# GQA decode attention with a gated MLP: the first block of wo by its own transfers in mid-run

## The chip, the core and the metric

The kernel runs on one NeuronCore of a Trainium2 chip. The metric is the device time of one execution in microseconds. Before the change it is 678.9 us, the median of three runs (678.57 to 679.03). The profiled execution took 678.28 us.

## What is computed

One token for each of 8 sequences goes through grouped-query attention over a cache, and the result is gated by an MLP:

```python
xn = layernorm(x)                                   # x: 8 x 1 x 512
q  = xn @ wq                                        # 32 heads of 128
p  = softmax(q . k_cache * 128 ** -0.5)             # 8 kv heads, 4096 keys each
s  = (p @ v_cache) as 8 x 4096, @ wo                # wo: 4096 x 512
g  = silu(gmlp(xn))                                 # w_in, spatial gate, w_out
out = x + s * g
```

All data is float32. The k and v caches are 8 x 8 x 4096 x 128 each, so nearly all of the 290.85 MB that a run moves is cache. wo is read as 32 blocks (one for each query head) of 128 rows x 512.

## The kernel before

Three slots of 128 x 16384 float32 (A, B, C) take all large arrays in turn. SyncE (SP) issues nearly all loads: wq into B, then for each of the 8 kv heads the two halves of k into A and B (`load_k`, L572) and the two halves of v into C and B (`load_v`, L577 and L578). A load waits on SP until the tensor engine has read the slot's last contents. ScalarE (ACT) issues x and w_mlp at the start. GpSimd issues no transfer: in the loop over the heads it only copies one head's q into `qz` (L524), and each of these copies waits for the previous head's output to be stored (L620).

For one head, the scores of all sequences are matmuls into PSUM (L531); a softmax over 128 x 1024 follows on VectorE and ScalarE; then the values (L563), whose diagonal blocks VectorE picks and sums (L565, L566), and a small matmul that puts them together (L569). The tensor engine and VectorE run these heads as a hardware loop; the other engines' programs are written out. A recorder notes every instruction with the regions that it reads and writes, and works out the waits: a matmul that reads a loaded block waits for the transfers that wrote it.

At the end wo goes into slot A in seven pieces, listed in `WO_PIECES` by block numbers and issued by L582, one semaphore each. Blocks 0 to 27 are multiplied by `folded_wo` (L590) into four row groups of PSUM, block by block as the pieces land; VectorE copies the sum out (L634), 16 small matmuls fold the row groups (L639), and blocks 28 to 31 are multiplied straight into the result's shape by `direct_wo` (L598). The gate and x follow on VectorE (L644, L645), and SP stores the result (L646).

A transfer of 128 rows is spread over the core's 16 DMA engines.

Of the kernel before, what the change touches and what calls it, by code (L numbers as in the profile page):

```python
# [15 lines left out]
P = 128  # L16
B, D = 8, 512
HKV, REP, S, DH = 8, 4, 4096, 128
# [3 lines left out]
R = 32  # L22
# [5 lines left out]
HALF = B // 2  # L28
UNIT = 2 * G * 512
SLOT = HALF * UNIT  # L30
WO_PIECES = [(0, 14), (14, 22), (22, 25), (25, 28), (28, 30), (30, 31), (31, 32)]
FOLDED = 28
FOLD_AT = 29
X_PARTS = 2
# [1 line left out]
XW = D + 64  # L36
E = 2
W = P // E
BANK = 512


class Region:


    def __init__(self, ap):
# [10 lines left out]
        if str(ap.space) == "PSUM" or "PSUM" in str(ap.space):  # L56
            self.p0, self.p1 = 0, P
            banks = np.unique(at // BANK)
            at = (banks[:, None] * BANK + np.arange(BANK)[None, :]).reshape(-1)
        at = np.unique(at)  # L60
# [279 lines left out]
        return self.rec.add(self.eng, "tensor_tensor", (out, a, b), {"op": ALU.subtract})  # L340


def gqa_gmlp_decode(real, x, kT, v, wq, wo, w_mlp, out):
    nc = Recorder(real)

    def sb(name, shape, **kw):
        return real.alloc_sbuf_tensor(name, shape, F32, **kw).ap()
# [51 lines left out]
    def shift(t, i):  # L399
        lo = (E - 1 - i) * B  # L400
        return t[:, lo:lo + R]
# [19 lines left out]

    gate, xg, wb = sb("gate", [P, W]), sb("xg", [P, W]), sb("wb", [P, 2])
    px = scr[1][:, :W + 2]
    for i in range(E):
        for g in range(G):
            lo = g * P + i * W
            nc.tensor.matmul(px[R * g:R * (g + 1), :W], shift(same8, i)[:B], x_sb[:, lo:lo + W],
                             start=(i == 0), stop=(i == E - 1))
    nc.tensor.matmul(px[:, W:], ones, xs_sb[0:1, D:D + 2], start=True, stop=True)
    nc.vector.tensor_copy(xg, px[:, :W])  # L430
    nc.vector.tensor_copy(wb, px[:, W:])
# [85 lines left out]
    oT = sb("oT", [P, FOLDED // REP, REP, B])  # L517
# [63 lines left out]
    def load_wo(lo, hi):  # L581
        nc.sync.dma_start(slots["A"][:, lo * D:hi * D], wo[:, lo * D:hi * D])  # L582

    wo_sb = slots["A"].rearrange("p (m d) -> p m d", d=D)
    part, acc = sc[:, 0, :], sc[:, 1, :W]

    def folded_wo(lo, hi):
        for m in range(lo, hi):
            h, r = divmod(m, REP)
            nc.tensor.matmul(part[R * r:R * r + B, :], oT[:, h, r, :], wo_sb[:, m, :],  # L590
                             start=(m < REP), stop=(m >= FOLDED - REP))

    def direct_wo(lo, hi):
# [8 lines left out]
    def head(h):  # L602
        spread_q(h)
        for half, n in enumerate("AB"):
            scores(half, load_k(h, half, n))
        softmax()
        for half, n in enumerate("CB"):
            v_sb, rest = load_v(h, half, n, 1 if h == HKV - 1 and half else 0)
            for i in range(HALF):
                b = half * HALF + i  # L610
                values(b, v_sb[:, i], rest if b == B - 3 else None)
                if b > 0:
                    combine(b - 1)
        combine(B - 1)
        if h < FOLDED // REP:
            to = oT[:, h]
        else:
            m = h * REP - FOLDED
            to = oT_end[:, m:m + REP, (E - 1) * B:E * B]
        nc.stored = nc.scalar.activation(to, po.rearrange("p (b r) -> p r b", r=REP), AF.Copy)  # L620
# [2 lines left out]
    project_q(1)  # L623
    mlp()
    nc.meet("tensor")
    for h in range(HKV):
        with nc.round(h):
            head(h)

    for lo, hi in WO_PIECES:  # L630
        load_wo(lo, hi)
    folded_wo(0, FOLDED)
    part_sb = pbuf[:, :D]
    nc.vector.tensor_copy(part_sb, part)  # L634
# [46 lines left out]
```

## Time and profile before

| what | value |
|---|---|
| median of 3 runs | 678.9 us (678.57 to 679.03) |
| profiled execution | 678.28 us |
| its span | 677.0 us |
| data moved | 290.85 MB, 430 GB/s over the span |
| PE busy | 373.0 us (55%) |
| VectorE busy | 164.9 us (24%) |
| GpSimd busy | 4.3 us (1%) |
| DMA packets | 6229, of which 6048 on SP's queue, 176 on ACT's, 5 for instructions |

The span is the time from the first to the last instruction in the profile. "q1" is SP's queue and "q10" ACT's. A DMA share of 1.00 means that all 16 DMA engines were at work throughout a stretch; 0.25 is four of them. PEclk is the tensor engine's granted clock as a share of full speed. A row of the timeline gives start, duration, engine, line, and in brackets the idle time before it and what ended it.

### The profile page before, as it was taken

How to read it: one execution, taken by the hardware profiler on the slowest of the kernel's cores; microseconds unless marked ns; L12 is line 12 of the kernel's file. 1: busy time of each engine (PE TensorE's matmuls, PEld its weight loads, DVE VectorE, ACT ScalarE, POOL GpSimd, SP SyncE). 2: the span in 40 equal slices, each digit the busy share in tenths (PEclk: the TensorE clock that was granted, in tenths of full speed). 3: DMA queues.
4: the chain of work that ended last, by engine and by line, in shares of the span. 5: the costliest groups of instructions: out<-in, count | busy, mean ns of one | idle time of the engine just before them, and what ended most of it. 6: DMA issues, size and time to landing. Idle time of an engine off the chain costs nothing. (4 is left out here: it accounts for less than half of the span.)

```text
span 677.0 us, 5987 instructions
## 1 busy us (share of the span) xinstructions
PE 373.0 (55%) x2570; PEld 118.4 (17%) x2570; DVE 164.9 (24%) x261; ACT 15.0 (2%) x35; POOL 4.3 (1%) x22
## 2 busy tenths in 40 slices
PE   0084864536665464555755355655745456755676
PEld 0021321112111121111211021111211121211222
DVE  2014042301440033401421024400422024400361
ACT  0000000000000000000000000000000000000000
POOL 1000000000000000000000000000000000000000
PEclk9996877888776667878767678876667788776697
DMA  9999999999999999999999999999999999999997
GB/s 382 446 429 434 435 434 434 435 434 434 434 434 434 434 434 434 434 434 434 434 434 434 434 434 434 434 434 434 434 434 434 434 434 434 434 434 434 453 413 314
DMA packets 6229, 290.85 MB, mean 430 GB/s; under 512 B 832, under 2 KB 848, under 8 KB 1488
## 3 DMA queue, kind: packets, MB, share of 16 engines
q1 hardware_dynamic: 6048, 285.25, 97.4%
q10 hardware_dynamic: 176, 5.52, 1.9%
q8 instruction: 4, 0.07, 0.0%
q14 instruction: 1, 0.01, 0.0%
HBM read 290.74 MB, written 0.03 MB: 430 GB/s over the span
## 5 line engine op out<-in xcount | busy, mean ns | idle before, releaser
L531 PE MATMUL sc<-slot_B,qz 128*32 128x512 f32 x512 | 71.6, 722 | 71.3 <-PEq L531 71.3
L563 PE MATMUL o_ps<-slot_B,tbuf 128*16 128x512 f32 x512 | 75.0, 712 | 63.4 <-PEq L563 63.4
L531 PE MATMUL sc<-slot_A,qz 128*32 128x512 f32 x512 | 72.6, 731 | 44.7 <-PEq L531 44.7
L563 PE MATMUL o_ps<-slot_C,tbuf 128*16 128x512 f32 x512 | 77.3, 746 | 13.9 <-PEq L563 13.9
L565 DVE TENSOR_TENSOR o_all<-o_ps,diag 128x512 f32<-128x512 f32 x64 | 44.2, 691 | 136.4 <-DVEq L565 135.5
L535 DVE TENSOR_REDUCE nm<-sc 128x1 f32<-128x1024 f32 x8 | 9.8, 1224 | 264.1 <-DVEq L535 264.1
L566 DVE TENSOR_REDUCE o_sb<-o_all 128x128 f32<-128x512 f32 x64 | 67.7, 1058 | 9.3
L531 PEld LDWEIGHTS sc<-slot_B,qz 128*32 128x32 f32 x512 | 20.4, 130 | 122.3 <-issue 122.3
L531 PEld LDWEIGHTS sc<-slot_A,qz 128*32 128x32 f32 x512 | 20.5, 131 | 90.2 <-issue 90.2
L569 PE MATMUL po<-fold,o_sb 128*128 128x4 f32 x128 | 24.4, 261 | 18.5 <-PEq L569 17.0
L569 PEld LDWEIGHTS po<-fold,o_sb 128*128 128x128 f32 x128 | 20.1, 198 | 73.9 <-issue 73.9
L563 PEld LDWEIGHTS o_ps<-slot_B,tbuf 128*16 128x16 f32 x512 | 13.3, 105 | 91.3 <-issue 90.8
L563 PEld LDWEIGHTS o_ps<-slot_C,tbuf 128*16 128x16 f32 x512 | 15.7, 113 | 56.3 <-issue 56.0
L553 PE MATMUL scr<-ident,pbuf 128*128 128x128 f32 x64 | 15.5, 424 | 13.4 <-PEq L553 13.4
L440 PE MATMUL scr<-slot_B,xnT 128*32 128x512 f32 x64 | 8.9, 706 | 19.5 <-PEq L440 19.5
L553 PEld LDWEIGHTS scr<-ident,pbuf 128*128 128x128 f32 x64 | 12.5, 223 | 13.8 <-issue 13.8
L536 ACT ACTIVATE pbuf<-sc,nm 128x1024 f32<-128x1024 f32 x8 | 8.9, 1113 | 271.4 <-DVEq L535 271.4
L554 DVE COPY tbuf<-scr 128x512 f32<-128x512 f32 x16 | 11.1, 691 | 12.3 <-DVEq L554 12.3
L590 PE MATMUL sc<-slot_A,oT 128*8 128x512 f32 x56 | 9.6, 801 | 1.6 <-DMA slot_A<-in_wo 1.6
L539 PE MATMUL scr<-ident,nm 128*1 128x128 f32 x8 | 2.2, 270 | 13.6 <-PEq L539 13.6
L442 DVE TENSOR_SCALAR pbuf<-scr 128x512 f32<-128x512 f32 x2 | 1.4, 692 | 27.6 <-PE scr L440 27.6
L546 PE MATMUL scr<-wl,same 128*128 128x1 f32 x16 | 3.2, 272 | 8.0 <-PEq L546 8.0
(100 smaller groups left out, 76.8 us busy)
## 6 DMA issues: line engine op xcount, KB each, us to landing
slot_B<-in_v SPq DMA_DIRECT2D x1, 6144.0 KB, 25.9
slot_C<-in_w_mlp ACTq DMA_DIRECT2D x1, 5376.0 KB, 40.6
slot_A<-in_wo SPq DMA_DIRECT2D x1, 3584.0 KB, 37.0
slot_B<-in_v SPq DMA_DIRECT2D x1, 2048.0 KB, 28.9
slot_A<-in_wo SPq DMA_DIRECT2D x1, 2048.0 KB, 41.3
slot_A<-in_wo SPq DMA_DIRECT2D x2, 768.0 KB, 43.4
slot_A<-in_wo SPq DMA_DIRECT2D x1, 512.0 KB, 44.9
slot_A<-in_wo SPq DMA_DIRECT2D x2, 256.0 KB, 45.1
```

The source lines that it names most:

```text
L440: nc.tensor.matmul(pq[R * g:R * (g + 1), :], xnT[:, k, :], wq_sb[:, k, lo:lo + REP * DH], start=(k == 0), stop=(k == NK - 1))
L531: nc.tensor.matmul(sc[R * g:R * (g + 1), c, :], qz[:, b * R:(b + 1) * R], k_sb[:, i, c, g, :], start=(b == 0), stop=(b == B - 1))
L535: nc.vector.tensor_reduce(nm, sc, op=ALU.max, axis=AX.XY, negate=True)
L536: nc.scalar.activation(p.rearrange("p j s -> p (j s)"), sc.rearrange("p c s -> p (c s)"), AF.Exp, bias=nm, accum_out=l)
L546: nc.tensor.matmul(tot, same_all, wl, start=True, stop=True)
L553: nc.tensor.transpose(t[:, j * P:(j + 1) * P], p[:, 4 * c + j, :], ident)
L554: nc.vector.tensor_copy(pT[:, :, 4 * c:4 * c + 4].rearrange("p b j (g r) -> p (j g) b r", g=G), t.rearrange("p (m b r) -> p m b r", b=B, r ...
L563: nc.tensor.matmul(of[R * c:R * c + G * REP, :], pT[:, b, j, :], v_unit[:, j], start=(j < G), stop=(j >= J - G))
L565: nc.vector.tensor_mul(o_all[b % 2], o, diag[:, :, None].to_broadcast([P, G, DH]), after=after)
L566: nc.vector.tensor_reduce(o_sb[b % 2], o_all[b % 2].rearrange("p g d -> p d g"), op=ALU.add, axis=AX.X)
L569: nc.tensor.matmul(po[:, b * REP:(b + 1) * REP], o_sb[b % 2], fold, start=True, stop=True)
L590: nc.tensor.matmul(part[R * r:R * r + B, :], oT[:, h, r, :], wo_sb[:, m, :], start=(m < REP), stop=(m >= FOLDED - REP))
```

## The change

Block 0 of wo no longer comes with the first piece. It has a place of its own, `wo_0` (128 x 512), and is brought in by three transfers that are issued ahead of head 4: on GpSimd one of 7 rows and one of 119 rows (seven times 17), and on SP one of the last 2 rows. For the GpSimd transfers the host packs block 0 a second time, as the array `wo_first`: seven lines that hold 17 rows each and, behind them, one row as two halves set apart. In GpSimd's program the two transfers stand between the copy of q for head 3 and that for head 4; in SP's, the third stands between the last load of v of head 3 and the first load of k of head 4. `folded_wo` reads block 0 from its new place.

```diff
-WO_PIECES = [(0, 14), (14, 22), (22, 25), (25, 28), (28, 30), (30, 31), (31, 32)]
+WO_PIECES = [(1, 14), (14, 22), (22, 25), (25, 28), (28, 30), (30, 31), (31, 32)]
...
+SK, SR, SH = 7, 17, 4
...
+    def wo_block(m):
+        return wo_sb[:, m, :] if m else wo_0
+
...
-            nc.tensor.matmul(part[R * r:R * r + B, :], oT[:, h, r, :], wo_sb[:, m, :],
+            nc.tensor.matmul(part[R * r:R * r + B, :], oT[:, h, r, :], wo_block(m),
                              start=(m < REP), stop=(m >= FOLDED - REP))
...
+    wo_0 = sb("wo_0", [P, D])
+
+    def load_first():
+        half = D // 2
+        nc.gpsimd.dma_start(wo_0[:SK], wo_first[:, SR * D:].rearrange("k (a d) -> k a d", a=2)[:, :, :half])
+        nc.gpsimd.dma_start(wo_0[SK:SK + SK * SR], wo_first[:, :SR * D].rearrange("k (r d) -> k r d", d=D))
+        nc.sync.dma_start(wo_0[SK + SK * SR:], wo[SK + SK * SR:, :D])
+
     for h in range(HKV):
+        if h == SH:
+            load_first()
         with nc.round(h):
             head(h)
...
+    first = wo[:, :D]
+    halves = np.zeros((SK, 2, D), np.float32)
+    halves[:, :, :D // 2] = first[:SK].reshape(SK, 2, D // 2)
+    wo_first = np.concatenate([first[SK:SK + SK * SR].reshape(SK, SR * D), halves.reshape(SK, 2 * D)], axis=1)
```

## Rows read from the trace of the kernel before

**Rows 1.** The page, parts 1 to 3: busy time, 40 slices, queues (packets, MB, share).
```profile
PE 373.0 (55%) x2570; PEld 118.4 (17%) x2570; DVE 164.9 (24%) x261; ACT 15.0 (2%) x35; POOL 4.3 (1%) x22
...
DMA  9999999999999999999999999999999999999997
GB/s 382 446 429 434 435 434 434 435 434 434 434 434 434 434 434 434 434 434 434 434 434 434 434 434 434 434 434 434 434 434 434 434 434 434 434 434 434 453 413 314
...
q8 instruction: 4, 0.07, 0.0%
```

**Rows 2.** The chain of waits in order of time: start us, us, what.
```profile
626.28 36.99 DMA slot_A<-in_wo
...
663.32 9.63 PE sc L590 x56
...
675.14 0.23 DVE res L645
```

**Rows 3.** Stretches at the last landing: engines' busy time, PEclk, DMA share, GB/s.
```profile
672.25:672.50 0.25, 0.25 (x6) 0.00 (x0) 0.00 (x0) 0.00 (x0) 0.00 (x0) 1.00 0.98 385
672.50:672.75 0.25, 0.25 (x3) 0.00 (x0) 0.00 (x0) 0.00 (x0) 0.00 (x0) 1.00 0.61 230
672.75:673.00 0.25, 0.16 (x3) 0.00 (x0) 0.03 (x1) 0.00 (x0) 0.00 (x0) 1.00 0.34 131
673.00:673.25 0.25, 0.04 (x4) 0.07 (x7) 0.25 (x1) 0.00 (x0) 0.00 (x0) 1.00 0.32 123
673.25:673.50 0.25, 0.25 (x16) 0.23 (x16) 0.25 (x1) 0.00 (x0) 0.00 (x0) 1.00 0.26 98
673.50:673.75 0.25, 0.18 (x15) 0.04 (x6) 0.16 (x1) 0.00 (x0) 0.00 (x0) 1.00 0.25 98
673.75:674.00 0.25, 0.25 (x20) 0.25 (x24) 0.00 (x0) 0.00 (x0) 0.00 (x0) 1.00 0.20 74
674.00:674.25 0.25, 0.25 (x34) 0.25 (x26) 0.00 (x0) 0.00 (x0) 0.00 (x0) 1.00 0.00 0
```

**Rows 4.** The DMA view from 49 to 51 us: queue, packets, MB, share of 16 engines.
```profile
q8 instruction: 1, 0.02, 3.0%
```

**Rows 5.** The page, part 6: DMA issues, KB, median us to landing.
```profile
slot_A<-in_wo SPq DMA_DIRECT2D x1, 3584.0 KB, 37.0
...
slot_A<-in_kT SPq DMA_DIRECT2D x8, 48.0
```

**Rows 6.** The timeline of GpSimd: start us, us, what, idle before and releaser.
```profile
281.88 0.21 POOL L524 COPY qz<-qT 128x32 f32<-128x32 f32 x1 [77.52 <-ACT oT L620]
359.77 0.21 POOL L524 COPY qz<-qT 128x32 f32<-128x32 f32 x1 [77.68 <-ACT oT L620]
```

**Rows 7.** The timeline of SP around the place of the third transfer.
```profile
316.06 0.33 SPq L577 DMA_DIRECT2D slot_B<-in_v  x1
316.43 0.43 SPq L572 DMA_DIRECT2D slot_A<-in_kT  x1
```

**Rows 8.** The timeline of PE's weight loads of L590: first and last.
```profile
663.31 0.12 PEld L590 LDWEIGHTS sc<-slot_A,oT 128*8 128x8 f32 x8 [1.73 <-DMA slot_A<-in_wo]
...
671.87 0.11 PEld L590 LDWEIGHTS sc<-slot_A,oT 128*8 128x8 f32 x6 [0.66 <-DMA slot_A<-in_wo]
```

**Rows 9.** Stretches from 661 to 672 us, columns as in Rows 3.
```profile
661.00:662.00 1.00, 0.36 (x2) 0.30 (x2) 0.17 (x1) 0.20 (x1) 0.00 (x0) 0.93 0.77 328
662.00:668.00 6.00, 4.68 (x24) 0.89 (x26) 0.00 (x0) 0.00 (x0) 0.00 (x0) 0.50 0.98 416
...
669.00:672.00 3.00, 3.00 (x29) 0.75 (x24) 0.00 (x0) 0.00 (x0) 0.00 (x0) 1.00 1.00 411
```

**Rows 10.** The DMA view from 2 to 30 us: queue, packets, MB, share.
```profile
q1 hardware_dynamic: 126, 7.73, 64.5%
q10 hardware_dynamic: 113, 4.14, 34.2%
```

More of the change, by code (lines that the diff above doesn't have):

```diff
@@ L340, in tensor_sub, with gqa_gmlp_decode @@
         return self.rec.add(self.eng, "tensor_tensor", (out, a, b), {"op": ALU.subtract})
-def gqa_gmlp_decode(real, x, kT, v, wq, wo, w_mlp, out):
+def gqa_gmlp_decode(real, x, kT, v, wq, wo, w_mlp, wo_first, out):
     nc = Recorder(real)
@@ L664 @@
         c(w_out.transpose(1, 0, 2)).reshape(P, NB * D)], axis=1)
+    wo = c(c(A_wo).reshape(HKV * REP, P, D).transpose(1, 0, 2)).reshape(P, SLOT)
+    first = wo[:, :D]
+    halves = np.zeros((SK, 2, D), np.float32)
+    halves[:, :, :D // 2] = first[:SK].reshape(SK, 2, D // 2)
+    wo_first = np.concatenate([first[SK:SK + SK * SR].reshape(SK, SR * D), halves.reshape(SK, 2 * D)], axis=1)
     arrays = {
@@ L669 @@
         "wq": c(c(A_wq).reshape(NK, P, HKV * REP * DH).transpose(1, 0, 2)).reshape(P, SLOT),
-        "wo": c(c(A_wo).reshape(HKV * REP, P, D).transpose(1, 0, 2)).reshape(P, SLOT),
+        "wo": wo,
         "w_mlp": w_mlp,
+        "wo_first": wo_first,
     }
```

## The prediction

> **What bounds the kernel now.** I read the page first: the DMA line is 9 in 39 of 40 slices at 434 GB/s, while PE is busy 55% of the span and no other engine more than 24% [rows 1]. Bytes set the time, so a change can win only where some of the 16 DMA engines stand still while others work. The chain of waits says where that is: from 626.28 the end hangs on the transfers of wo for 36.99 us, then 9.63 us of matmuls of L590, and 2.4 us, up to 675.37, of fold, last blocks, gate and residual [rows 2]. Next I read the stretch around the last landing in quarter-microseconds. The DMA share is 0.98 until 672.50, then 0.61, 0.34, 0.32, 0.26, 0.25, 0.20, and nothing after 674.00 [rows 3]. A share of 0.25 is 4 of 16 engines. So some eleven engines are through by about 672.8, a twelfth soon after, and four work alone until about 674.0. Spread evenly, the same work (0.25 us times 2.96, the sum of the shares from 672.25 on: 0.74 us) would end at 673.0: at most 1.0 us is to be had here.
>
> Who are the four? Four packets of the instruction queue (0.07 MB together, some 16 KB each) stand beside the data in the whole span [rows 1]; one of them, at 49 to 51 us, took 3.0% of 16 engines over 2 us, 0.96 us of one engine [rows 4]. That four such packets made four engines late is an inference: no view names the engine of a packet.
>
> **The change part by part.** One engine moves 434/16 = 27.1 GB/s [rows 1]; a row of block 0 is 2 KB and takes it 0.075 us.
>
> Removed: block 0 leaves the first piece of wo, 256 of 3584 KB [rows 5]. Each engine carries 8 of the 128 rows, 16 KB, so each is through 0.60 us sooner. The seven issues on SP stay seven at 0.43 us.
>
> Added on GpSimd: two transfers, behind the copy of head 3 at 281.88 and before that of head 4, which begins at 359.77 after 77.68 us of waiting [rows 6]. Nothing else is queued there; whatever an issue costs POOL (no row shows one; between nothing and those 77 us) is covered. Block 0 is needed at 661, so some 340 us are left for it; 0 on the path.
>
> Added on SP: the last two rows, between the load of 316.06 and that of 316.43, at some 0.43 us [rows 7]. The load behind it is one of kT into slot A (128 x 16384 f32, 8.4 MB); the median of these lands 48.0 us after its issue [rows 5], though its bytes need only 19.3 us at 434 GB/s. The difference, 29 us, is work queued ahead of it. 0 on the path.
>
> Moved between engines: seven get 17 rows, 17 x 0.075 = +1.28 us, less the 0.60 removed: +0.68. Seven get one row, +0.08, and two of those one more: -0.53 or -0.45. Two get nothing: -0.60. If the four late engines are all among the nine with little, they end at 674.00 - 0.53 = 673.5, and the seven loaded ones at 672.8 + 0.68 = 673.5 at the latest. The last data lands 0.5 us sooner. [...]
>
> Does that reach the end? The last weight loads of L590, at 671.87, waited 0.66 us for their piece [rows 8], so TensorE has room there, and the piece comes 0.5 earlier. Before it, L590 begins at 663.31 on the first piece, which also comes 0.5 earlier, and block 0 is multiplied by then, in the idle time before it (1.73 us of waiting, [rows 8]). [...] The extra waits of block 0 (three transfers, not one) fall into idle time: 0.
>
> The one price that is not in a row is what a packet from GpSimd's queue costs an engine beyond its bytes. From below: 0. While ACT's queue ran beside SP's from 2 to 30 us, 113 of its packets lay between 126 of SP's, and the two shares make 98.7% of all engine time [rows 10]. From above: the instruction packet took 0.96 us for bytes worth some 0.6 [rows 4], and if it made its engine late by the 1.2 to 1.4 us by which the four outlast the others, it cost up to 0.8 beyond its bytes. I take 0, since ACT's packets are also loads into the core's memory between SP's packets, and are many; both ends go into the range.
>
> Sum, on the profiled execution (678.28 us with a span of 677.0): -0.5, so 677.8. The median of the three runs is 678.9, 0.6 above it; on that the forecast is **678.4 us**, with its own range from 677.9 (the whole 1.0) to 678.7 (0.3 lost to the clock).
>
> **Rivals.**
> *A late engine is among the loaded seven.* Four late engines and nine lightened ones of 16 leave room for it, and no view names an engine. Then that engine ends at 674.0 + 0.68, the tail grows by 0.7: 679.6 us. This is slower than before though within what can be told. It decides as soon as one late engine gets 17 rows.
>
> *The rows are not spread as described.* If the 119 rows go 8 to an engine, as all others do, every engine carries what it carried: the tail keeps its shape, but each engine's share of block 0 has only moved from the end to mid-run, where the engines are busy too: 678.9 us. The change would then have moved bytes and no balance. Against it: the two added transfers read with three dimensions (7 x 2 x 256 and 7 x 17 x 512), whose outer 7 argues for seven engines. [...]
>
> *A change of queue costs each time (the other side).* Place: the seven engines with 17 rows, at about 282 to 320 us; price: the 0.8 us above. SP's queue is never empty, so an engine may go back to it after each row. Decides: once a loaded engine is more than 0.5 us later than summed, so already with one such cost. If paid once per engine (its rows in one go), the loaded ones end at 673.5 + 0.8, 0.3 after today's end: 679.2 us. If paid for each of 17 rows, 13.6 us: 673.5 + 13.6 is 13.1 after today's end, 692.0 us; for every second one (9 times, 7.2 us), 685.6. For it: the excess of the instruction packet. Against it: ACT's 113 packets without any [rows 4, 10].
>
> **How the numbers follow.** Chances: forecast 0.50; late engine among the loaded 0.18; not spread 0.12; queue cost paid once 0.11; paid many times 0.09. Within 0.2% is 1.36 us to either side of 678.9, about what a measurement here can tell from no change. The first four lie within it; a gain beyond it would need more than the 1.0 us that the tail holds, 0.03 (taken from the forecast). Slower beyond it: the last, and 0.01 for a late engine that also pays a queue cost, 0.10. Same 0.87. The range takes in the first four: from 677.7 (the whole tail, and the scatter of the runs, some 0.2 to either side) to 680.0 (a loaded engine that an instruction packet makes 1.4 late: 673.5 + 1.4, 0.9 after today's end, 679.8, and scatter); it leaves out the many-times case.
>
> **What would show it.** Right: in the last two microseconds of data, the share falls from about 1 to nothing within 1 us and not 1.5; the first piece lands near 36.4 us and not 37.0; L590 begins half a microsecond earlier; the DMA line stays at 434 GB/s around 282 to 330 us, where a new queue stands with about 0.25 MB. Seven engines, not four, should make up the last stretch. Wrong: a tail in which one to four engines work longer than before (late among the loaded), an unchanged tail (not spread), a slice or two below 430 GB/s near 300 us and a long tail at a share of 0.44, seven engines (queue costs). A new instruction packet beside the GpSimd issues would make one more engine late and take the gain away.

## The result, and the profile after

The changed kernel takes 680.44 us, the median of 22 runs (680.10 to 685.99), against 678.58 us (678.31 to 679.03) for the kernel before in the same series: a ratio of 1.003, with a 95% interval of 1.0023 to 1.0037. It is 1.9 us slower, where 0.5 us less was forecast. Its profiled execution took 680.59 us with a span of 679.3.

The page, parts 2 and 3, against [rows 1]:

```profile
GB/s 388 442 422 433 433 433 433 432 432 432 436 436 448 444 440 432 433 395 422 436 436 440 432 432 432 432 432 432 432 432 432 432 432 436 440 436 440 418 424 300
DMA packets 6426, 290.85 MB, mean 428 GB/s; under 512 B 957, under 2 KB 973, under 8 KB 1685
...
q0 software_dynamic: 192, 0.26, 0.1%
q8 instruction: 4, 0.07, 0.0%
```

Where every slice in the middle of [rows 1] stood at 434, two now stand at 395 and 422, from 289 to 323 us. That is where the new queue q0, GpSimd's, has its 192 packets. The issues themselves are as cheap and as well covered as predicted ([rows 6] showed GpSimd waiting there, [rows 7] SP's place):

```profile
283.01 0.75 POOL L635 DMA_DIRECT2D wo<-in_wo_first  x1
283.76 0.66 POOL L636 DMA_DIRECT2D wo<-in_wo_first  x1
```

```profile
320.39 0.34 SPq L637 DMA_DIRECT2D wo<-in_wo  x1
```

The first piece of wo is smaller, and yet lands as long after its issue as in [rows 5]:

```profile
slot_A<-in_wo SPq DMA_DIRECT2D x1, 3328.0 KB, 37.0
```

The chain of waits, against [rows 2] (start us, us, what), now hangs on a late piece and not on the first:

```profile
630.09 44.09 DMA slot_A<-in_wo
674.18 0.04 issue
674.23 1.07 PE sc L595 x6
...
677.50 0.22 DVE res L660
```

In [rows 8] the last weight loads began at 671.87; these six matmuls begin at 674.23, 2.4 us later, which is the whole loss of the profiled execution (680.59 against 678.28, 2.3 us). The stretches at the last landing show who is late; the last two columns are DMA share and GB/s, as in [rows 3]:

```profile
673.50:674.00 0.50, 0.00 (x0) 0.00 (x0) 0.00 (x0) 0.00 (x0) 0.00 (x0) 1.00 0.86 332
674.00:674.50 0.50, 0.27 (x3) 0.11 (x6) 0.00 (x0) 0.00 (x0) 0.00 (x0) 1.00 0.71 275
674.50:675.00 0.50, 0.50 (x6) 0.00 (x0) 0.00 (x0) 0.00 (x0) 0.00 (x0) 1.00 0.56 217
675.00:675.50 0.50, 0.26 (x3) 0.00 (x0) 0.18 (x1) 0.00 (x0) 0.00 (x0) 1.00 0.09 33
675.50:676.00 0.50, 0.43 (x16) 0.30 (x16) 0.50 (x1) 0.00 (x0) 0.00 (x0) 1.00 0.06 25
676.00:676.50 0.50, 0.43 (x31) 0.43 (x35) 0.01 (x1) 0.00 (x0) 0.00 (x0) 1.00 0.04 16
```

The balancing works for most: eleven engines on average are busy from 674.0 on (a share of 0.71) and nine in the next half microsecond (0.56), and they end together at about 675.0. But 0.06 is one engine of 16, and it works alone until about 676.3. Two things are to be explained: the dip near 300 us, and the one engine.

### The profile page after: what moved, and what is told of

Its sections match the earlier page's. It is cut to its first block, busy times and chain, and to the rows that moved or that the text cites. A ratio compares the mean times of both kernels' runs of the same rounds, so it can differ in the third digit from the quotient of the medians.

```text
span 679.3 us, 5991 instructions
## 1 busy us (share of the span) xinstructions
PE 374.7 (55%) x2570; PEld 117.8 (17%) x2570; DVE 165.0 (24%) x261; ACT 15.0 (2%) x35; POOL 5.7 (1%) x24
## 5 line engine op out<-in xcount | busy, mean ns | idle before, releaser
L564 PE MATMUL o_ps<-slot_B,tbuf 128*16 128x512 f32 x512 | 76.7, 726 | 63.6 <-PEq L564 63.6
L532 PE MATMUL sc<-slot_A,qz 128*32 128x512 f32 x512 | 74.6, 747 | 44.3 <-PEq L532 44.3
L595 PE MATMUL sc<-slot_A,oT 128*8 128x512 f32 x54 | 7.5, 593 | 2.0 <-DMA slot_A<-in_wo 2.0
```

The costliest lines, as they stand in the source:

```text
L532: nc.tensor.matmul(sc[R * g:R * (g + 1), c, :], qz[:, b * R:(b + 1) * R], k_sb[:, i, c, g, :], start=(b == 0), stop=(b == B - 1))
L564: nc.tensor.matmul(of[R * c:R * c + G * REP, :], pT[:, b, j, :], v_unit[:, j], start=(j < G), stop=(j >= J - G))
```

## Experiments

Where a median is given with "before", the latter is from the same series. The trace also has each packet's start and duration, though no view lists them. From these I read, for two loads on SP's queue, at 277 and 606 us of the trace's own clock (about 11 us ahead of the span's), when the first and the last of the 16 engines ended, and how much later the second is than in the kernel before. The column "lost by all" is this delay of the first engine to end, less the 0.60 us of block 0's bytes where every engine carries 8 rows of it; elsewhere nothing is taken off, as the first to end carries no row or one (0.08 us).

```
kernel                    first   last - first   lost by all   time, before (us)
before                    0       1.62           -
changed kernel           +1.75    2.71           1.75          680.44, 678.58
e1 SP, 128 rows          +0.63    1.72           0.02          678.70, 678.60
e2 GpSimd, 128 rows      +0.61    1.67           0.00          678.49, 678.60
e3 SP, change's split    +1.42    3.15           1.42          680.92, 678.60
f1 SP, 128, own copy     +0.62    1.58           0.02          678.70, 678.51
f2 SP, 2 x 64 rows       +1.73    1.77           1.13          679.89, 678.51
f3 SP, split, from wo    +1.64    2.98           1.64          680.92, 678.51
f4 GpSimd, engines 6-12  +1.37    1.33           1.37          680.63, 678.51
g1 SP, 2 half widths     +0.67    1.57           0.06          678.70, 678.61
g3 64 extra, together    +0.51    2.48           0.51          679.97, 678.61
g4 GpSimd, engines 7-12  +1.14    1.55           1.14          679.28, 678.61
h1 64 extra, four apart  +0.05    2.27           0.05          679.32, 678.66
h2 64 extra, together    +0.42    2.48           0.42          679.82, 678.66
```

What the end should cost is the first column, plus the growth of the second over 1.62, less 0.60 where block 0 left the tail. For the change that is 1.75 + 1.09 - 0.60 = 2.24 us, against 2.31 measured in the profiled execution and 1.86 between the medians; between the medians also, e3 has 2.35 against 2.32, f2 1.28 against 1.38, h2 1.28 against 1.16. In all rows but one the two columns give the loss to within 0.4 us, in most to within 0.2; the one is f4 (0.48 against 2.12), which is taken up below.

**e1, e2, e3: the queue or the split.** My first theory laid the dip on GpSimd's queue.

```diff
 e1
-  nc.gpsimd.dma_start(wo_0[:SK], wo_first[:, SR * D:].rearrange("k (a d) -> k a d", a=2)[:, :, :half])
-  nc.gpsimd.dma_start(wo_0[SK:SK + SK * SR], wo_first[:, :SR * D].rearrange("k (r d) -> k r d", d=D))
-  nc.sync.dma_start(wo_0[SK + SK * SR:], wo[SK + SK * SR:, :D])
+  nc.sync.dma_start(wo_0, wo[:, :D])
 e2 (the same lines go)
+  nc.gpsimd.dma_start(wo_0, wo[:, :D])
 e3 (of these, the two first)
+  nc.sync.dma_start(wo_0[:SK], wo_first[:, SR * D:].rearrange("k (a d) -> k a d", a=2)[:, :, :half])
+  nc.sync.dma_start(wo_0[SK:SK + SK * SR], wo_first[:, :SR * D].rearrange("k (r d) -> k r d", d=D))
```

> Block 0 comes in at the same place mid-run into wo_0, but as one transfer of 128 rows on SP; nothing on GpSimd's queue. Theory A (GpSimd's queue costs all 16 engines some 1.5 us while its transfers are in flight, and one late engine is among the loaded seven, 1.1 us at the end, less the 0.6 us of bytes that left the tail): both costs are gone and the bytes have only moved, 678.6 us (678.3 to 678.9), the tail of four late engines as before. Theory B (only the late engine costs): 678.6 too. Theory C (the place of its own, three waits instead of one or the move to mid-run costs): stays near 680.4.

> Block 0 as one transfer of 128 rows on GpSimd's queue, 8 rows for each engine, at the same place. Theory A: no engine is loaded more than another, and the common cost goes with the rounds in flight: 4 packets of two rows for each engine where the change had 9, so some 0.7 us: 679.3 us (679.0 to 679.6); data packets of SP's queue below 434 GB/s for some 12 us near 300 us. Theory B: 678.6 us, no dip. Theory C: 680.4.

> The change's own three transfers, all on SP. The rows are still dealt to seven engines, but which seven may differ (both of SP's transfers start at the first engine). Theory A: no dip at 300 us; the tail depends on whether a late engine is among the first seven: with one of 1.4 to 1.6 us among them 679.3 us (679.0 to 679.6), with none 678.1. Theory B: the same as A if the seven hold a late engine, as it lays all of the loss on that: 680.4. Theory C: 680.4.

Measured: e1 678.70 us (ratio 1.0001, 0.9992 to 1.0010), e2 678.49 (0.9998, 0.9989 to 1.0007), e3 680.92 (1.0035, 1.0022 to 1.0047), above every figure expected of it. The theory falls twice: GpSimd's queue costs nothing with an even split, and the split costs as much on SP. A stretch of 30 us shows it for the two GpSimd kernels (last column GB/s), first the change, then e2:

```profile
287.00:317.00 30.00, 16.01 (x108) 4.52 (x112) 0.00 (x0) 0.00 (x0) 0.00 (x0) 0.70 1.01 413
```

```profile
287.00:317.00 30.00, 17.43 (x128) 4.87 (x128) 0.00 (x0) 0.00 (x0) 0.00 (x0) 0.76 1.00 433
```

The DMA share is 1.0 in both: the engines are not idle, their packets take longer. In the change a 64 KB packet of SP's queue takes up to 2.8 us in this stretch, on all 16 engines, and 2.42 elsewhere (the median). The place of its own and a wait for it cost nothing either (e1, where block 0 comes by one transfer).

**e4: which engine is which.** Small transfers of 1 to 15 rows were added to the change ahead of head 2.

```diff
+  for k in range(1, 16):
+      n = 16 + 4 * k
+      nc.sync.dma_start(probe[:k, lo:lo + n], wo[:k, lo:lo + n])
...
```

> The changed kernel with 15 small transfers on SP ahead of head 2, of 1 to 15 rows and 80 to 304 bytes a row, to tell from the trace's packets which engine is which. Expected: transfers of k rows show k packets, on the first k engines, and the seven loaded engines are numbers 7 to 13 with one late engine among them; the same dip near 300 us as in the change. Time 680.5 to 681.5, not used.

A transfer of k rows had k packets. The late engines stand apart in the trace and can be followed (late by how much, at 150 us, against the engine that is furthest ahead). Each of them carries a row in all transfers from some k on, so as far as these four show, SP deals every transfer from the same engine on; k - 1 is an engine's number here:

```
late by   since                              rows in transfers of   engine
1.76 us   instruction packet, 16 KB, 1st     14, 15                 13
1.69      instruction packet, 16 KB, 2nd     15                     14
1.51      instruction packet, 16 KB, 3rd     6 to 15                5
1.07      instruction packet, 8 KB           4 to 15                3
```

So each late engine is one that an instruction packet met. Followed in the change's own trace, the engine of the first such packet, at 62 us, carries 17 rows of q0, that of the second (89 us) none, and those of the third (115 us) and of the 8 KB one (103 us) one row each: number 13 is among the loaded. I take the loaded seven to be 7 to 13; no packet names its engine. f4, in which one row fewer comes ahead of the seven shares, fits that: the lag of the last engine falls from 2.71 to 1.33 us. Time 680.66 us, as expected.

**f1, f2, f3: source or target of the rows.**

```diff
 f1 (against e1; wo_first is here a plain copy of block 0)
-  nc.sync.dma_start(wo_0, wo[:, :D])
+  nc.sync.dma_start(wo_0, wo_first)
 f2 (against e1)
-  nc.sync.dma_start(wo_0, wo[:, :D])
+  for at in (0, P // 2):
+      nc.sync.dma_start(wo_0[at:at + P // 2], wo[at:at + P // 2, :D])
 f3 (against e3)
-  nc.sync.dma_start(wo_0[SK:SK + SK * SR], wo_first[:, :SR * D].rearrange("k (r d) -> k r d", d=D))
+  nc.sync.dma_start(wo_0[SK:SK + SK * SR], wo[SK:SK + SK * SR, :D].rearrange("(k r) d -> k r d", k=SK))
```

> Block 0 mid-run as one SP transfer of 128 rows, read from a copy of its own whose rows lie end to end in memory (in wo they lie 64 KB apart). What the runs so far leave: the seven-engine split costs all 16 engines 1.3 to 1.6 us on either queue, and a late engine among the loaded costs another 1.1 us. Theory P (it matters which engine writes which rows of the core's memory: a row brought by another engine than the one that serves these rows in all other loads takes time from that one): even split, own rows, 678.6 us. Theory S (reading the repacked array is slow, as its rows lie together): some 1.3 to 1.6 us more, 680.0. Theory L (nothing but the late engine costs): 678.6.

> [...] Theory S and theory L: 678.6.

> The change's split on SP (as in the earlier run), with the 119 rows read from wo in place of the repacked array. Theory P: nothing changes against that run, 680.9 us (680.5 to 681.2). Theory S: only the late engine is left, 679.6. Theory L: 680.9, but with no loss on the engines that are not loaded.

Measured: f1 678.70 us (1.0002, 0.9993 to 1.0011), f2 679.89 (1.0019, 1.0010 to 1.0028), f3 680.92 (1.0034, 1.0021 to 1.0048). The source has no part in it. f2 is the telling one: each engine carries 8 rows, as many as in e1, and none falls behind the others (1.77 us from first to last, 1.62 before), yet all lose 1.1 us. The stretch where SP's transfers land, in e1, f2 and f3:

```profile
340.00:350.00 10.00, 3.90 (x18) 0.91 (x18) 0.11 (x1) 0.00 (x0) 0.00 (x0) 0.57 1.04 446
```

```profile
340.00:350.00 10.00, 3.04 (x16) 0.56 (x16) 0.00 (x0) 0.00 (x0) 0.00 (x0) 0.51 0.96 360
```

```profile
340.00:350.00 10.00, 3.02 (x16) 0.55 (x16) 0.00 (x0) 0.00 (x0) 0.00 (x0) 0.62 0.97 347
```

446 GB/s in e1, where block 0 comes by one transfer of 128 rows, 360 and 347 in f2 and f3, where its rows are dealt otherwise, with the engines busy nearly all the time (DMA share 0.96 and 0.97). These rates are coarse, as a packet counts whole where it starts and 16 packets of 64 KB are 105 GB/s of such a stretch. With each packet's bytes spread over its duration the three are 432, 383 and 367: 11 and 15% less for 10 us, about the 1.1 and 1.6 us of the table.

**f4 and g4: the late engine.** The loaded engines are moved off number 13.

```diff
 f4 (6 rows, then 119, then 3 on SP; wo_first packed to suit)
-  SK, SR, SH = 7, 17, 4
+  SK, SR, SH, S1 = 7, 17, 4, 6
...
-  nc.gpsimd.dma_start(wo_0[SK:SK + SK * SR], wo_first[:, :SR * D].rearrange("k (r d) -> k r d", d=D))
+  nc.gpsimd.dma_start(wo_0[S1:S1 + SK * SR], wo_first[:, :SR * D].rearrange("k (r d) -> k r d", d=D))
...
 g4 (7 rows, then 6 times 20, then 1 on SP)
-  SK, SR, SH = 7, 17, 4
+  SK, SR, SH, K2 = 7, 20, 4, 6
-  nc.gpsimd.dma_start(wo_0[SK:SK + SK * SR], wo_first[:, :SR * D].rearrange("k (r d) -> k r d", d=D))
+  nc.gpsimd.dma_start(wo_0[SK:SK + K2 * SR], wo_first[:K2, :SR * D].rearrange("k (r d) -> k r d", d=D))
...
```

> The change with 6 rows in the first GpSimd transfer in place of 7 (and 3 on SP in place of 2), so that the 17-row shares fall on engines 6 to 12 and not 7 to 13. By the probe's packets the late engines are 13, 14, 5 and 3, none of them among the loaded now. Theory P: the common loss of 1.3 to 1.6 us stays, the 1.1 us of the late engine goes: 679.3 us (679.0 to 679.6). Theory L: all of the loss goes and the gain of the prediction shows: 678.1. Theory S: as P, 679.3. If the loaded seven are not where the probe puts them: 680.4.

> The change with six engines loaded (7 to 12, 20 rows each) in place of seven; the 7 single rows before them on GpSimd and 1 row on SP stay. Engines 13, 14, 5 and 3 are late by mid-run and a fourth instruction packet in the tail falls, by the last run, on engine 6: none of these is loaded now. Theory P: the common loss of some 1.3 us stays, no engine stands alone at the end: loaded engines end 0.9 later by bytes, late ones 0.6 sooner, so 0.8 us more than before: 679.4 us (679.0 to 679.8). If the late loaded engine was all there was to the change's loss (theory L): 678.3. If engines matter not at all: 680.4.

f4 measured 680.63 us (680.33 to 681.79; 1.0032, 1.0020 to 1.0044), a miss: 679.3 was expected, and 680.4 only if the loaded engines were not where the probe puts them. But the spread of its loads did shrink (1.33 against 2.71), and only at the end does one engine work alone again:

```profile
674.50:675.00 0.50, 0.50 (x3) 0.00 (x0) 0.00 (x0) 0.00 (x0) 0.00 (x0) 0.50 0.40 152
675.00:675.50 0.50, 0.50 (x6) 0.00 (x0) 0.00 (x0) 0.00 (x0) 0.00 (x0) 0.50 0.06 25
675.50:676.00 0.50, 0.50 (x10) 0.47 (x10) 0.00 (x0) 0.00 (x0) 0.00 (x0) 0.50 0.06 25
```

A fourth instruction packet, 0.02 MB on q8, comes during the tail, between 665 and 670 us; engine 6, which f4 adds to the loaded ones, is where I take it to fall (an inference, as no packet names its engine). This profile also has PEclk at 0.50 there, after TensorE had waited 1.74 us for a piece: L654 and L603 took 0.66 and 0.78 us, against 0.43 and 0.71 in the change, and the execution 681.79. g4 leaves out both 6 and 13 and measured 679.28 us (1.0010, 1.0001 to 1.0019), as expected, with no lone engine:

```profile
673.50:674.00 0.50, 0.47 (x6) 0.00 (x0) 0.00 (x0) 0.00 (x0) 0.00 (x0) 1.00 0.75 287
674.00:674.50 0.50, 0.25 (x16) 0.28 (x16) 0.47 (x1) 0.00 (x0) 0.00 (x0) 1.00 0.69 266
674.50:675.00 0.50, 0.40 (x30) 0.24 (x23) 0.22 (x1) 0.00 (x0) 0.00 (x0) 1.00 0.49 188
675.00:675.50 0.50, 0.50 (x52) 0.50 (x44) 0.00 (x0) 0.00 (x0) 0.00 (x0) 1.00 0.00 0
```

Most of the engines now end together, as the prediction drew it (0.69 is eleven of 16), though the share takes 1.5 us to fall to nothing, where it had said 1. All of it comes later, for the 1.14 us that all engines lost.

**g1, g2, g3, h1, h2: which rows, or small transfers.**

```diff
 g1 (against e1, in place of its one transfer)
+  for at in (0, half):
+      nc.sync.dma_start(wo_0[:, at:at + half], wo[:, at:at + half])
 g2, h1 (kernel before, with 64 rows read once more, unused; in g2 and g3 without the t % 4)
+  for t in range(8):
+      lo = 32 * (t // 4) + t % 4
+      nc.sync.dma_start(own[lo:lo + 29:4, t % 4, :], wo[lo:lo + 29:4, :D])
 g3, h2
+  for t in range(8):
+      lo = 8 * t
+      nc.sync.dma_start(own[lo:lo + 8, t % 4, :], wo[lo:lo + 8, :D])
...
```

g2 and h1 take eight rows that lie 4 apart in each transfer, g3 and h2 eight that lie together. Theory P has the former as rows that the same engines write in the large loads, and most of the latter as rows of other engines; that is my assumption and not shown, as no packet names its engine or its rows.

> Block 0 mid-run on SP from wo, as two transfers of all 128 rows and half the width each, where the run before had two of 64 rows. Theory P (a row of the core's memory that another engine than its usual one writes takes time from all): every engine writes its usual rows, 678.6 us (678.3 to 678.9). Rival N (two transfers or small packets are what costs): 679.5 to 679.9, as with the halves.

> The kernel before with 64 more rows read in mid-run that the result does not use (rows 0 to 63 of block 0, 128 KB, read again into a place of its own; VectorE reads that place once before the tail). [...] Theory P: 16 KB more on eight engines and nothing else, +0.6 us at the late one among them: 679.1 us (678.8 to 679.4). Rival N: 680 or more, as there are eight small transfers.

> [...] Theory P: 0.5 to 1.5 us above the run of own rows, 679.6 to 680.6 us, and the loss is seen on all engines, those without extra rows too. Rival N: the same time as the run of own rows.

> [...] Theory P (the loss comes when an engine writes other rows than its usual ones): only 16 KB more on engines 0 to 7, +0.6 us at the late one among them and nothing on the others: 679.1 us (678.9 to 679.4). Rival N (many small transfers cost): as the next run.

> [...] Theory P: as the earlier run of other rows, 680.0 us (679.7 to 680.3), with 0.5 us lost by engines that carry none of it. Rival N: the same time as the run of own rows.

g1 measured 678.70 us (1.0000, 0.9991 to 1.0009): two transfers of smaller packets cost nothing. g2 was spoiled at 694.50 (1.0233, 1.0219 to 1.0247), as its transfers waited for each other on SP:

```profile
SPq L631 <- DMA own<-in_wo: 35.5, 6, 28.3
```

g3 gave 679.97 (1.0021, 1.0012 to 1.0030). The clean pair is h1, 679.32 (1.0011, 1.0002 to 1.0020), and h2, 679.82 (1.0017, 1.0008 to 1.0026). Both intervals against the kernel before overlap; set against each other, the eleven times of h1 (679.13 to 679.65) and of h2 (679.50 to 680.08) hardly do. What h1 loses is not lost by all (0.05): eight engines carry 8 rows more, 0 to 7 by the probe's numbers, and two of them, 3 and 5, are late. The same 10 us in h1 and then h2:

```profile
340.00:350.00 10.00, 3.85 (x18) 0.86 (x18) 0.06 (x1) 0.00 (x0) 0.00 (x0) 0.55 1.01 433
```

```profile
340.00:350.00 10.00, 3.27 (x16) 0.55 (x16) 0.00 (x0) 0.00 (x0) 0.00 (x0) 0.57 0.96 393
```

433 GB/s against 393 by this coarse view (g3 has 433 too), 431 against 413 with the bytes spread over the packets' durations (g3: 409). The packets themselves are plainer: three of 64 KB in h1 take longer than 2.42 us there, by at most 0.2; in h2 every engine, with extra rows or without, has one or two that take 0.3 to 0.6 us longer together.

## Why the prediction was wrong

*What bounds the kernel, and the tail.* Right. [rows 3] held four late engines, and the probe bears out the inference of [rows 4] that instruction packets make them late: three by mid-run, beside a smaller one of 8 KB, and one in the tail. In g4 the end comes 0.67 us later where all engines lost 1.14, so the tail itself is 0.5 shorter, as was summed for the change.

*Removed, issues, waits.* Right: in e1, moving block 0 into its own place, with a wait for it, changes nothing (678.70). The clock did no harm in the change, with PEclk at 1.00 in the stretches above and from 660 us to them. The 0.3 us that the range allows for it no run shows; the one profile with PEclk at 0.50 at the end, f4's, took 1.2 us more than the median of its runs (681.79, 680.63).

*Moved between engines.* The deal of the rows is right: q0 has seven engines with 17 rows each (eight packets of two rows and one of one), so the rival "not spread" is out. The condition "if the four late engines are all among the nine with little" failed: one late engine, number 13, carries 17 rows. That rival stood at 679.6 with a chance of 0.18; its price was +0.68, and the packets give 1.09 - 0.60 = 0.49 on top of what all engines lost; g4, without a late engine among the loaded, is 1.2 us below the change.

*The price beyond the bytes, taken as 0: the step that failed most.* I had looked for it in a change of queue, on the loaded engines only, up to 0.8 us a time. The sign that was to show it came, slices of 395 and 422 GB/s near 300 us, but the price hangs neither on the queue nor on the loaded engines alone: e2 has GpSimd's queue and loses nothing, e3 and f3 have no GpSimd transfer and lose 1.4 to 1.6 us. It is paid by all 16 engines, those with no row too, by 0.42 to 1.75 us (the column "lost by all") in the change, e3, f2, f3, f4, g3, g4 and h2, and by 0.06 at most in e1, e2, f1 and g1, which bring block 0 by transfers of 128 rows, and in h1, whose transfers take rows four apart (f2 and h2 against g1 and h1 are the plainest pairs). The sum had let bytes move freely from one engine to another. That the price is paid where rows are written by other engines than in the large loads is theory P: these runs fit it, but none shows which engine writes which row. Why such a deal holds up all engines, and not only those that carry the rows, no run here shows either. Nor does the price go by the number of extra rows alone: 64 cost all engines 0.05 us in h1 and 0.42 in h2, and block 0's 128 cost 0.02 in e1 and 1.13 in f2.

The loss of the change is thus 1.75 us for all and 0.5 for the late engine (1.09 - 0.60); the sum had 0 and -0.5. No version was found that beats the kernel before: the two deals that were to spare late engines cost all engines 1.37 us (f4) and 1.14 (g4), and g4, the best found, still loses 0.7 us.

## What to carry to other kernels

In a stream that filled all DMA engines, bytes could not be dealt from a late engine to others at the price of the bytes: rows dealt otherwise than by transfers of 128 slowed every engine, by 0.4 to 0.5 us for 64 rows of 2 KB (h2, g3) and 1.1 to 1.75 us for 128 (f2, and the change at the upper end). The one exception is h1, whose transfers of 8 rows four apart cost all engines 0.05 us. Before a transfer is reshaped, run it evenly on the same queue and reshaped on another one; two runs, such as e2 and e3, would have shown here that the shape costs time and the queue does not. Where engines are late, find out by number which ones, and count those that will be late by the end too.

## What was not expected of the hardware

- Transfers of GpSimd's queue were cut into packets of up to two 2 KB rows (56 of 4 KB and 14 of 2 KB in the change), and 81 of q0's 192 packets hold 8 bytes (82 in f4, 109 in g4, none in e2, where every engine has rows). The counts fit small packets for the engines that carry no row of a transfer; no view names a packet's engine. Beside SP's full queue the 0.26 MB took some 28 us, and 12 us in e2's even split, as one packet of rows went between two of 64 KB.
- An instruction packet of 16 KB, worth 0.6 us of bytes, held its engine 0.88 to 0.97 us and made its next 64 KB packet 0.47 to 0.55 longer: some 1.4 us in all, never made up in a run at full rate (in the kernel before, these engines stand as far behind at 290 us as at 150, to 0.02 us). There were three before the tail and one in it, on four engines if the last fell on engine 6.
